# Weight conversion behind the first maxima, MLP's Relu and squares half a step later, and head 6's sums ahead of head 7's

## The chip, the cores and the metric

The kernel runs on one NeuronCore of a Trainium2 chip. Its engines are TensorE (PE, the matrix unit), VectorE (DVE), ScalarE (ACT), GpSimd (POOL), and SyncE (SP), which issues most of the DMAs. The metric is the device time of one launch in microseconds; below, a median of three runs.

## The reference

Eight batches of eight heads of attention with a decay, over 576 positions of 64 channels, are followed by an MLP on the 4608 tokens of 512 channels:

```python
scores = scale * np.matmul(q, k.transpose(0, 1, 3, 2))
cum = np.cumsum(np.log(np.clip(f, 0.0001, 1.0)), axis=-1)
decay = cum[:, :, :, None] - cum[:, :, None, :]
scores = np.where(causal, -1000000000.0, scores + decay)
scores = scores - np.max(scores, axis=-1, keepdims=True)
attn = np.exp(scores)
attn = attn / (np.sum(attn, axis=-1, keepdims=True) + 1e-09)
x = np.matmul(attn, v)                    # then heads beside each other: 4608 x 512
h = np.maximum(x @ w_in, 0.0)             # 512 x 2048, weights given in float64
out = h * h @ w_out                       # 2048 x 512
```

## The kernel before, in words

The work of the 64 heads is cut into units, six a head (`NU`): each is one block of scores against up to 448 queries, its exponential, and, two units later (`LAG`), its product with the values. Unit `n` is the step of one long traced loop, from `-12` to the end; what a unit issues on PE, ACT, DVE and POOL stays in exactly the order in which the loop wrote it (`in_order`, L18). So an instruction that waits holds up everything behind it on its engine. SP's DMAs are placed by the scheduler.

A softmax row's maximum is computed one head ahead, by six pieces of scores (`max_units`, L363) that DVE reduces (L380). A piece's PSUM bank is free for another product when L380 is done. For the first ten heads the maxima are then turned on PE (`turn_maxima`, L403) and copied by ACT (L407) into a row of the operand of the scores, which run in full float32 there (L419); from head 10 on the scores are made of two rounded products (L421, L424), and from head 16 on the probabilities are split too: ACT casts (L451), DVE subtracts (L452), and PE makes three products (L462 to L464) into one accumulator bank that ACT empties (L497, L498). POOL masks those probabilities (L438).

The sums of a pair of heads are inverted and spread through DMAs (`finish`, L500), and POOL multiplies (L519). Only for heads 6 and 7, the last of the first batch, is this done on PE and DVE at once (`finish_here`, L523): one-column matmuls (L533) turn the sums into columns, DVE inverts, and matmuls against an identity (L548) spread them.

The 32 weight tiles are given in float64. Each is loaded by SP (L195), made a float32 by ACT (magnitude, L206) and DVE (L229, L234, L237, L240), and split into a high part (ACT, L211) and a low part (DVE, L217). `weight_ops` (L187) is a generator whose yields are steps, four to a weight; `RATES` (L654) says how many steps each unit takes: first number for units -12 to -7, second for -3 to -1, third to the unit at which the first batch is ready (53), fourth from there until all are done.

The MLP runs in half steps that `fill` (L690) spreads over the units by a goal that depends on the unit's number alone. An even half (`mlp1`, L576) makes one 128 x 256 block of `x @ w_in` from twelve matmuls (L582) into the single bank 4, then Relu on ACT (L590), the square twice, on DVE (L591) and rounded on ACT (L592), and their difference on DVE (L593). An odd half (`mlp2`, L596) makes the second product of the step before by six matmuls (L605). Twelve matmuls on constants before the first score (`spin`, L751) and 36 at the very start keep PE's clock up.

While the first two chunks of the MLP share the weights that are ready, scores and maxima have two PSUM banks; from the third chunk on they have four.

Of the kernel before, what the change touches and what calls it, by code (L numbers as in the profile page):

```python
# [9 lines left out]
F32 = mybir.dt.float32  # L10
# [24 lines left out]
def decay_attention_relu2_kernel(  # L35
# [18 lines left out]
    nc = tc.nc  # L54

    NH, D, _, S = qk.shape
    P = 2 * D
# [26 lines left out]
    def bank(use):  # L84

        turn = banks[use] or banks["s"]
        b = turn.pop(0)
        turn.append(b)
        return psum.tile([P, 512], F32, name=f"bank{b}")
# [97 lines left out]
    def weight_ops():  # L187

        staged, done = {}, {}

        def stage():
            i = len(staged)
            if i < NW:
                raw = staged[i] = wk.tile([P, 2 * DM], I32, name=f"w{i}", bufs=1)
                nc.sync.dma_start(out=raw, in_=(w_in, w_out)[i % 2][i // 2].bitcast(I32))  # L195

        def words(i):
            w = staged[i].rearrange("p (n t) -> p n t", t=2)
            return w[:, :, 0], w[:, :, 1]

        mags = {}

        def magnitude(i):
            if i < NW:
                mags[i] = wk.tile([P, DM], F32, name="wmag", bufs=1)
                nc.scalar.activation(out=mags[i], in_=words(i)[1].bitcast(F32), func=AF.Abs)  # L206

        def high_part(i):
            if i >= 0:
                hl = wk.tile([P, 2, DM], F32R, name=f"w{i}", bufs=1)  # L210
                nc.scalar.copy(out=hl[:, 0], in_=done[i])  # L211
                done[i] = done[i], hl

        def low_part(i):
            if i >= 0:
                w, hl = done.pop(i)
                nc.vector.tensor_tensor(out=hl[:, 1], in0=w, in1=hl[:, 0].bitcast(F32), op=ALU.subtract)  # L217
                split_w.append(hl)

        stage()  # L220
        yield
        magnitude(0)
        stage()
        yield
        for i in range(NW):
            low, high = words(i)
            mag = mags.pop(i)

            nc.vector.tensor_scalar(mag, mag, MAG_LOW, MAG_HIGH, ALU.max, ALU.min)  # L229
            yield  # L230
            w = done[i] = wk.tile([P, DM], F32, name="osb")
            wi = w.bitcast(I32)

            nc.vector.tensor_scalar(wi, mag.bitcast(I32), 3, 0x3FFFFFFF, ALU.logical_shift_left, ALU.bitwise_and)  # L234
            high_part(i - 1)
            yield
            nc.vector.scalar_tensor_tensor(wi, high, -0x40000000, wi, ALU.bitwise_and, ALU.bitwise_or)  # L237
            magnitude(i + 1)
            yield
            nc.vector.scalar_tensor_tensor(wi, low, 29, wi, ALU.logical_shift_right, ALU.bitwise_or)  # L240
            low_part(i - 1)
            while len(staged) < min(i + 1 + DEPTH, NW):
                stage()
            yield
        high_part(NW - 1)
        yield
        low_part(NW - 1)
        yield
# [271 lines left out]
            del state[h], state[h - 1]  # L520


    def finish_here(h, part):  # L523

        st = state[h]
        cuts = [min(j * P, S - P) for j in range(NJ)]
        if part == 0:
            one = vhs[0][:, 0, D:D + 1].bitcast(F32)
            c = st["cmp"] = wk.tile([P, 2 * NJ], F32, name="cmp")
            for i in range(2):  # L530
                ps = bank("m")
                for j, q0 in enumerate(cuts):
                    nc.tensor.matmul(  # L533
                        ps[:, j:j + 1], st["den"][i * D:i * D + 1, q0:q0 + P],
                        one[i * D:i * D + 1], start=True, stop=True,
                    )
                nc.vector.tensor_scalar_add(c[:, i * NJ:(i + 1) * NJ], ps[:, :NJ], EPS)
            nc.vector.reciprocal(out=c, in_=c)
        if part == 1:
            c = st["cmp"]  # L540
            x = xts[h // H][:, (h % H) // 2, :]
            for a, b in ((0, 512), (512, S)):
                ps = bank("m")
                for j, q0 in enumerate(cuts):
                    if a <= j * P < b:
                        m = min(S - j * P, P)
                        for i in range(2):
                            nc.tensor.matmul(  # L548
                                ps[i * D:(i + 1) * D, j * P - a:j * P - a + m],
                                c[:, i * NJ + j:i * NJ + j + 1].broadcast_to([P, D]),  # L550
                                eye_r[:, P - m:].bitcast(F32), start=True, stop=True,
                            )
                nc.vector.tensor_tensor(out=x[:, a:b], in0=x[:, a:b], in1=ps[:, :b - a], op=ALU.mult)
            del state[h], state[h - 1]
# [3 lines left out]
    def split_x(c, finished):  # L558
# [14 lines left out]
            t0 = t1  # L573
        mst["x", c] = (xh, xl), t0

    def mlp1(c, fc):  # L576
        xh, xl = mst["x", c][0]
        ph = bank("h")
        w = split_w[2 * fc].rearrange("p s (c f) -> p s c f", f=P)
        for k, (s, x) in enumerate(((1, xh), (0, xh), (0, xl))):  # L580
            for cc in range(NCC):
                nc.tensor.matmul(  # L582
                    ph[:, :T], w[:, s, cc], x[:, cc, :],
                    start=(cc == 0 and k == 0), stop=(cc == NCC - 1 and k == 2),
                )
        r = wk.tile([P, T], F32, name="r", bufs=1)
        g = wk.tile([P, T], F32, name="g", bufs=1)
        gh = wk.tile([P, T], F32R, name="gh")
        gl = wk.tile([P, T], F32R, name="gl")
        nc.scalar.activation(out=r, in_=ph[:, :T], func=AF.Relu)  # L590
        nc.vector.tensor_tensor(out=g, in0=r, in1=r, op=ALU.mult)  # L591
        nc.scalar.activation(out=gh, in_=r, func=AF.Square)  # L592
        nc.vector.tensor_tensor(out=gl, in0=g, in1=gh.bitcast(F32), op=ALU.subtract)  # L593
        mst["g", c, fc] = (gh, gl)
# [30 lines left out]
                return None  # L625

    def mlp_half(finished):
        if halves[0] % 2:
            if len(steps) > 1:
                mlp2(*steps[-2])  # L630
# [20 lines left out]

    RATES = (1, 1.6, 0.8, 1.8)  # L654
    LAG = 2
    NA = H * NU

# [21 lines left out]
    fins = {}  # L679
    for h in range(1, NH, 2):  # L680
        if h == H - 1:
            for part in range(2):
                fins.setdefault((h + 1) * NU + 2 + part, []).append((finish_here, h, part))
            continue
        for part in range(4):
            fins.setdefault(fin(h, part), []).append((finish, h, part))
# [75 lines left out]
    load_cum(0, rounded[0].k)  # L762
    load_cum(0, whole[0].k, D + 1)
    store_cum()
    load_rounded(1, False)
    load_whole(1)
    load_cum(1, rounded[1].k)
# [26 lines left out]
    convert(1 << 20)  # L794
    while halves[0] < 2 * NCHUNK * NF:
        mlp_half(B)
    mlp2(*steps[-1])
    in_order(tc, [getattr(mybir.EngineType, e) for e in ("PE", "Activation", "DVE", "Pool")], start)

# [38 lines left out]
```

## Time and profile before

| | us |
|---|---|
| median of three runs (1216.88 to 1219.87) | 1217.59 |
| profiled execution, its own time | 1216.4 |
| its span, first to last instruction | 1214.7 |
| PE busy | 1182.6 (97%) |
| DVE busy | 784.1 (65%) |
| ACT busy | 696.0 (57%) |
| POOL busy | 304.6 (25%) |
| granted PE clock, mean | 0.99 |

Busy time of PE is modelled, since matmuls overlap; what a matmul really takes of PE is read from the distance of starts. A row of the timeline gives start and duration in us, the engine (PEld is PE's weight load, SPq an issue of a DMA), the line, the operation, output and inputs by the program's names, and in brackets the idle time of the engine before it and what ended it. Line numbers in rows of the profile before are those of the kernel before.

### The profile page before, as it was taken

To read this page: it belongs to the slowest core of one execution; us is meant where nothing else is said; L and a number is where in the kernel's file an instruction comes from. 1 tells how busy PE (TensorE), PEld (TensorE's weight loads), DVE (VectorE), ACT (ScalarE), POOL (GpSimd) and SP (SyncE) were. 2 spreads that over 40 slices of the span, in tenths; PEclk is the share of its full clock that TensorE was granted. 3 is DMA by queue.
4 is the path that set the end of the run, shared out by engine and by line. 5 is a ranking of instruction groups with operands and counts; after the bars stand their busy time and mean duration, and the time that the engine had idled before them with its cause. 6 is when DMAs were issued, how large, how long until landed. Compare 5 with 4: busy or idle time off the path is not lost. (4 is left out here: it accounts for less than half of the span.)

```text
span 1214.7 us, 23295 instructions
## 1 busy us (share of the span) xinstructions
PE 1182.6 (97%) x7786; PEld 1043.8 (86%) x7786; DVE 784.1 (65%) x2095; ACT 696.0 (57%) x1716; POOL 304.6 (25%) x511
## 2 busy tenths in 40 slices
PE   6999999989999999999999999999999999999998
PEld 3668777779998899999999989998899899999997
DVE  5878888666666767665655766667666667533332
ACT  2875555546665666656556566666666666533232
POOL 2110000113334333322322333333333333200000
PEclk8998999989999999999999999999999999999999
DMA  7785522221212111121120211212121212000000
GB/s 214 201 229 173 137 52 55 69 53 42 59 42 54 41 50 42 42 54 24 42 59 16 54 34 48 51 42 60 36 55 32 54 42 59 11 28 10 9 19 18
DMA packets 109799, 73.33 MB, mean 60 GB/s; under 512 B 90720, under 2 KB 90720, under 8 KB 109680
## 3 DMA queue, kind: packets, MB, share of 16 engines
q1 hardware_dynamic: 108880, 68.90, 22.1%
q0 software_dynamic: 800, 2.95, 1.0%
q8 instruction: 62, 1.02, 0.3%
q14 instruction: 57, 0.47, 0.1%
HBM read 58.71 MB, written 9.87 MB: 56 GB/s over the span
## 5 line engine op out<-in xcount | busy, mean ns | idle before, releaser
L605 PE MATMUL bank<-w,gh 128*128 128x512 f32 x1152 | 414.0, 400 | 0.0
L582 PE MATMUL bank<-xh,w 128*128 128x256 f32 x2304 | 329.9, 286 | 1.6 <-ACT w L211 1.6
L582 PEld LDWEIGHTS bank<-xh,w 128*128 128x128 f32 x2304 | 301.6, 190 | 9.8 <-ACT w L211 2.2
L452 DVE TENSOR_TENSOR pl<-p,ph 128x320 fp32r<-128x320 f32 (+4 forms) x288 | 175.6, 610 | 193.4 <-ACT ph L451 188.2
L605 PEld LDWEIGHTS bank<-w,gh 128*128 128x128 f32 x1152 | 217.5, 189 | 38.4
L590 ACT ACTIVATE r<-bank 128x256 f32<-128x256 f32 x288 | 110.4, 383 | 221.5 <-PE bank L582 183.3
L605 PE MATMUL bank<-w,gl 128*128 128x512 f32 x576 | 227.0, 394 | 0.2 <-DVE gl L593 0.2
L591 DVE TENSOR_TENSOR g<-r 128x256 f32<-128x256 f32 x288 | 123.9, 430 | 134.2 <-ACT r L590 133.3
L451 ACT CAST ph<-p 128x320 fp32r<-128x320 f32 (+4 forms) x288 | 119.4, 415 | 145.2 <-POOL p L438 103.3
L582 PE MATMUL bank<-xl,w 128*128 128x256 f32 x1152 | 184.4, 282 | 0.0
L438 POOL TENSOR_SCALAR_AFFINE_SELECT p<-p 128x128 f32<-128x128 f32 (+1 forms) x240 | 77.3, 322 | 423.2 <-ACT p L436 328.9
L582 PEld LDWEIGHTS bank<-xl,w 128*128 128x128 f32 x1152 | 158.2, 191 | 0.0
L593 DVE TENSOR_TENSOR gl<-g,gh 128x256 fp32r<-128x256 f32 x288 | 126.8, 440 | 35.0 <-PE bank L605 0.5
L436 ACT ACTIVATE p<-bank 128x320 f32<-128x320 f32 (+4 forms) x288 | 111.4, 387 | 64.6 <-PE bank L424 52.8
L380 DVE CUSTOM_DVE_ANT_0 bank<-bank,mz 128x256 f32<-128x256 f32 (+4 forms) x320 | 133.3, 432 | 18.6 <-PE bank L372 17.1
L372 PE MATMUL bank<-rk 66*128 66x320 f32 (+4 forms) x384 | 110.7, 317 | 22.6 <-DVE tcol L380 16.3
L592 ACT ACTIVATE gh<-r 128x256 fp32r<-128x256 f32 x288 | 120.5, 418 | 9.2
L605 PEld LDWEIGHTS bank<-w,gl 128*128 128x128 f32 x576 | 109.2, 190 | 14.4 <-DVE gl L593 0.9
L372 PEld LDWEIGHTS bank<-rk 66*128 66x128 f32 (+1 forms) x384 | 67.3, 181 | 40.5 <-DVE tcol L380 21.2
L424 PE MATMUL bank<-rl 128*128 128x320 f32 x324 | 95.2, 294 | 0.0
L462 PE MATMUL bank<-pl,vh 128*65 128x320 f32 (+4 forms) x336 | 93.1, 277 | 1.9 <-ACT den L498 1.9
L421 PE MATMUL bank<-rk 67*128 67x320 f32 x324 | 93.4, 288 | 0.1
(97 smaller groups left out, 1483.8 us busy)
## 6 DMA issues: line engine op xcount, KB each, us to landing
qkraw<-in_qk SPq DMA_DIRECT2D x54, 288.0 KB
v<-in_v SPq DMA_DIRECT2D x64, 160.0 KB
out<-osb SPq DMA_DIRECT2D x36, 256.0 KB
den<-rdr SPq DMA_DIRECT2D x62, 144.0 KB
w<-in_w_in SPq DMA_DIRECT2D x16, 512.0 KB
w<-in_w_out SPq DMA_DIRECT2D x16, 512.0 KB
rk<-tcol SPq DMA_DIRECT2D x216, 0.5 KB
rl<-in_qk SPq DMA_DIRECT2D x10, 288.0 KB
```

The source lines that it names most:

```text
L372: nc.tensor.matmul(ps[:m, :n], st["r2"][:D + 2, q0:q0 + m], st["kl0"][:D + 2, k0:k0 + n], start=True, stop=True,)
L380: nc.vector.tensor_tensor_reduce(out=ps[:m, :n], in0=ps[:m, :n], in1=mz[:m, mo:mo + n], op0=ALU.add, op1=ALU.min, scale=-1.0, scalar=init, ...
L424: nc.tensor.matmul(ps[:kn, :n], st["l2"][:, k0:k0 + kn], st["r1"][:, q0:q1], start=False, stop=not added,)
L436: nc.scalar.activation(out=p[:kn, :n], in_=ps[:kn, :n], func=AF.Exp, scale=SCALE)
L451: nc.scalar.copy(out=ph[:kn, :n], in_=p[:kn, :n])
L452: nc.vector.tensor_tensor(out=pl[:kn, :n], in0=p[:kn, :n], in1=ph[:kn, :n].bitcast(F32), op=ALU.subtract,)
L582: nc.tensor.matmul(ph[:, :T], w[:, s, cc], x[:, cc, :], start=(cc == 0 and k == 0), stop=(cc == NCC - 1 and k == 2),)
L590: nc.scalar.activation(out=r, in_=ph[:, :T], func=AF.Relu)
L591: nc.vector.tensor_tensor(out=g, in0=r, in1=r, op=ALU.mult)
L592: nc.scalar.activation(out=gh, in_=r, func=AF.Square)
L593: nc.vector.tensor_tensor(out=gl, in0=g, in1=gh.bitcast(F32), op=ALU.subtract)
L605: nc.tensor.matmul(po, g[:, ts], w[:, s], start=(fc == 0 and k == 0), stop=(fc == NF - 1 and k == 2),)
```

## The change

Four edits. The second weight is staged a step earlier, ahead of the loads of head 1, by one call more of `convert`; its magnitude is taken a step later, after the first weight's last bit operation (L240, now L242); and the rates are changed, so that the steps ahead of the first score become 4 instead of 10.8 and those between it and unit 53 more. `mlp1` only issues its matmuls; Relu, squares and difference are moved into `bend`, which the next half step calls first. In `finish_here` each head's sums are now a part of their own: head 6's at unit 46, head 7's at unit 50, the spreading at unit 51 as before.

```diff
@@ weight_ops
         stage()
         yield
+        stage()
+        yield
         magnitude(0)
-        stage()
         yield
@@ in its loop over the weights
-            magnitude(i + 1)
+            if i:
+                magnitude(i + 1)
             yield
             nc.vector.scalar_tensor_tensor(wi, low, 29, wi, ALU.logical_shift_right, ALU.bitwise_or)
             low_part(i - 1)
+            if i == 0:
+                magnitude(1)
@@ finish_here
-        if part == 0:
+        if part < 2:
             one = vhs[0][:, 0, D:D + 1].bitcast(F32)
-            c = st["cmp"] = wk.tile([P, 2 * NJ], F32, name="cmp")
-            for i in range(2):
-                ps = bank("m")
-                for j, q0 in enumerate(cuts):
-                    nc.tensor.matmul(
-                        ps[:, j:j + 1], st["den"][i * D:i * D + 1, q0:q0 + P],
-                        one[i * D:i * D + 1], start=True, stop=True,
-                    )
-                nc.vector.tensor_scalar_add(c[:, i * NJ:(i + 1) * NJ], ps[:, :NJ], EPS)
+            if part == 0:
+                inv.append(wk.tile([P, 2 * NJ], F32, name="cmp"))
+            c = inv[0][:, part * NJ:(part + 1) * NJ]
+            ps = bank("m")
+            o = part * D
+            for j, q0 in enumerate(cuts):
+                nc.tensor.matmul(
+                    ps[:, j:j + 1], st["den"][o:o + 1, q0:q0 + P], one[o:o + 1], start=True, stop=True,
+                )
+            nc.vector.tensor_scalar_add(c, ps[:, :NJ], EPS)
             nc.vector.reciprocal(out=c, in_=c)
-        if part == 1:
+        if part == 2:
@@ mlp1, after its matmuls: what follows is bend's now
+        bent.append((c, fc, ph))
+
+    def bend():
+
+        if not bent:
+            return
+        c, fc, ph = bent.pop()
         r = wk.tile([P, T], F32, name="r", bufs=1)
...
     def mlp_half(finished):
+        bend()
         if halves[0] % 2:
...
-    RATES = (1, 1.6, 0.8, 1.8)
+    RATES = (0.67, 0, 0.93, 1.8)
...
-            for part in range(2):
-                fins.setdefault((h + 1) * NU + 2 + part, []).append((finish_here, h, part))
+            for part, n in enumerate((h * NU + 4, (h + 1) * NU + 2, (h + 1) * NU + 3)):
+                fins.setdefault(n, []).append((finish_here, h - (part == 0), part))
...
     store_cum()
+    convert(1)
     load_rounded(1, False)
```

How it moves instructions is seen at three places. The first is DVE ahead of the first maximum (L380 before, L384 now; `wmag` is the magnitude, `osb` the float32 being made, `tcol` the maximum). Before:

```order
L229 TENSOR_SCALAR wmag<-wmag 128x512
L234 TENSOR_SCALAR osb<-wmag 128x512
L237 SCALAR_TENSOR_TENSOR osb<-w_143,osb 128x512
L240 SCALAR_TENSOR_TENSOR osb<-w_143,osb 128x512
L229 TENSOR_SCALAR wmag<-wmag 128x512
L380 ISA bank_187,tcol<-bank_187,mz 128x256
L380 ISA tcol 128x1
```

Now:

```order
L230 TENSOR_SCALAR wmag<-wmag 128x512
L235 TENSOR_SCALAR osb<-wmag 128x512
L238 SCALAR_TENSOR_TENSOR osb<-w_143,osb 128x512
L384 ISA bank_177,tcol<-bank_177,mz 128x256
L384 ISA tcol 128x1
L384 ISA bank_181,p<-bank_181,mz,tcol 128x320
```

L240 of the first weight and L229 of the second no longer stand ahead of head 0's maxima; they come after the first pieces of head 1's.

The second is DVE at head 12's first maximum, while weights are converted (`g` and `gl` are the square and the difference of the MLP; L325 is a part of the operands' preparation, L329 now). Before:

```order
L318 CAST rk_79<-qkraw 64x576
L229 TENSOR_SCALAR wmag<-wmag 128x512
L234 TENSOR_SCALAR osb<-wmag 128x512
L591 TENSOR_TENSOR g<-r 128x256
L593 TENSOR_TENSOR gl<-g,gh 128x256
L325 TENSOR_TENSOR rl<-qkraw,rk_79 64x576
L380 ISA bank_1672,tcol<-bank_1672,mz 128x256
L380 ISA tcol 128x1
L237 SCALAR_TENSOR_TENSOR osb<-w_1369,osb 128x512
```

Now:

```order
L322 CAST rk_79<-qkraw 64x576
L230 TENSOR_SCALAR wmag<-wmag 128x512
L607 TENSOR_TENSOR g<-r 128x256
L609 TENSOR_TENSOR gl<-g,gh 128x256
L235 TENSOR_SCALAR osb<-wmag 128x512
L329 TENSOR_TENSOR rl<-qkraw,rk_79 64x576
L384 ISA bank_1665,tcol<-bank_1665,mz 128x256
L384 ISA tcol 128x1
L238 SCALAR_TENSOR_TENSOR osb<-w_1349,osb 128x512
```

The pair `g`, `gl` ahead of the maximum belongs to the product that left PE just before, in the first listing, and to the one before that, in the second, where L235 (L234 before) has come behind it.

The third is ACT in head 20, from its fourth unit's exponential (66 x 64) to its sixth's (128 x 256); `r` and `gh` are the MLP's Relu and rounded square. Before:

```order
L436 ACTIVATE p<-bank_3812 66x64
L451 CAST ph<-p 66x64
L590 ACTIVATE r<-bank_3838 128x256
L592 ACTIVATE gh<-r 128x256
L436 ACTIVATE p<-bank_3859 128x448
L451 CAST ph<-p 128x448
L436 ACTIVATE p<-bank_3887 128x256
L451 CAST ph<-p 128x256
```

Now:

```order
L440 ACTIVATE p<-bank_3813 66x64
L455 CAST ph<-p 66x64
L440 ACTIVATE p<-bank_3852 128x448
L455 CAST ph<-p 128x448
L606 ACTIVATE r<-bank_3839 128x256
L608 ACTIVATE gh<-r 128x256
L440 ACTIVATE p<-bank_3888 128x256
L455 CAST ph<-p 128x256
```

Relu and rounded square went behind the exponential and the cast of the 448-wide unit. On PE nothing else changes its place but the one-column matmuls of `finish_here`; on POOL nothing does. On SP the second weight's load moves ahead of head 1's.

More of the change, by code (lines that the diff above doesn't have):

```diff
@@ L520, in finish @@
             del state[h], state[h - 1]
+    inv = []
     def finish_here(h, part):
@@ L526, in finish_here @@
         cuts = [min(j * P, S - P) for j in range(NJ)]
-        if part == 0:
+        if part < 2:
             one = vhs[0][:, 0, D:D + 1].bitcast(F32)
-            c = st["cmp"] = wk.tile([P, 2 * NJ], F32, name="cmp")
-            for i in range(2):
-                ps = bank("m")
-                for j, q0 in enumerate(cuts):
-                    nc.tensor.matmul(
-                        ps[:, j:j + 1], st["den"][i * D:i * D + 1, q0:q0 + P],
-                        one[i * D:i * D + 1], start=True, stop=True,
-                    )
-                nc.vector.tensor_scalar_add(c[:, i * NJ:(i + 1) * NJ], ps[:, :NJ], EPS)
+            if part == 0:
[8 more added lines that the diff above has]
+            nc.vector.tensor_scalar_add(c, ps[:, :NJ], EPS)
             nc.vector.reciprocal(out=c, in_=c)
-        if part == 1:
-            c = st["cmp"]
+        if part == 2:
+            c = inv[0]
             x = xts[h // H][:, (h % H) // 2, :]
@@ L574, in split_x @@
         mst["x", c] = (xh, xl), t0
+    bent = []
     def mlp1(c, fc):
@@ L796, in decay_attention_relu2_kernel @@
         mlp_half(B)
+    bend()
     mlp2(*steps[-1])
```

## The prediction

> **What bounds the kernel now.** I read the busy times by stage first, then who waits for whom on TensorE (PE), then the timeline at each place so found. A row of the first view gives a stretch in us, its length, busy us and instructions of PE, of PE's weight loads, of DVE, ACT and POOL, the granted PE clock and the DMA share. The last row is from the chain of waits.
>
> ```profile
> 12.38:15.79 3.41, 0.75 (x4) 0.28 (x3) 0.00 (x0) 0.00 (x0) 0.00 (x0) 1.00 0.64 156
> 15.79:26.03 10.24, 5.64 (x20) 3.33 (x20) 5.66 (x18) 2.54 (x5) 0.69 (x2) 0.50 0.89 299
> 25.35:86.49 61.14, 59.69 (x346) 41.13 (x345) 50.24 (x158) 47.06 (x117) 9.35 (x18) 0.99 0.82 210
> 90.88:97.71 6.83, 6.83 (x39) 5.17 (x35) 4.79 (x8) 1.96 (x5) 0.20 (x2) 0.50 0.41 161
> 244.48:247.89 3.41, 1.80 (x10) 1.24 (x9) 3.08 (x6) 1.10 (x4) 0.43 (x3) 1.00 0.00 0
> 263.27:1058.00 794.73, 790.82 (x5386) 721.05 (x5385) 530.61 (x1432) 502.25 (x1250) 271.49 (x430) 1.00 0.19 44
> 1206.63 1.43 PE bank L582 x12
> ```
>
> From 263 us on PE is busy for 790.8 of 794.7 us, and the chain shows twelve 256-column matmuls passing in 1.43 us, 0.119 each. That part is bound by PE's own work, which the change leaves alone. What can be won lies ahead of 263 us, where the waits of PE stand (us in total, times, longest); the second row is the first one confined to 90 to 270 us.
>
> ```profile
> PE bank L372 <- DVE tcol L380: 16.3, 7, 7.1
> PE bank L372 <- DVE tcol L380: 9.2, 6, 1.8
> PE bank L582 <- ACT w L211: 1.6, 1, 1.6
> PE bank L372 <- DVE rk L318: 1.6, 1, 1.6
> DVE g L591 <- ACT r L590: 133.3, 109, 2.4
> ```
>
> One wait of 7.1 us lies at the start, six make 9.2 us while weights are converted beside the first MLP chunks, and DVE itself stands 133 us behind the MLP's Relu.
>
> **The start: conversion leaves the first maxima's way.**
>
> ```profile
> 11.80 0.36 PE L372 MATMUL bank<-rk 66*128 66x256 f32 x1 [1.25 <-DMA rk<-qkraw]
> 14.78 0.36 SPq L195 DMA_DIRECT2D w<-in_w_out  x1
> 18.68 0.66 ACT L206 ACTIVATE wmag<-w 128x512 f32<-128x512 f32 x1 [10.65 <-DMA w<-in_w_out]
> 19.37 0.43 DVE L229 TENSOR_SCALAR wmag<-wmag 128x512 f32<-128x512 f32 x1 [8.52 <-ACT wmag L206]
> 19.71 0.43 DVE L380 CUSTOM_DVE_ANT_0 bank<-bank,mz 128x256 f32<-128x256 f32 x1
> 22.54 0.76 PE L403 MATMUL bank<-p 128*65 128x128 f32 x5
> 23.11 2.45 PE L751 MATMUL bank<-mz 128*128 128x448 bf16 x6
> 23.33 0.68 ACT L407 COPY rl<-bank 1x512 f32<-1x512 f32 x2 [3.99 <-PE bank L403]
> 25.35 1.04 PE L419 MATMUL bank<-rl 67*128 67x320 f32 x2
> ```
>
> Head 0's first maximum could run at 11.80 + 0.36 = 12.16, but on DVE it stands behind L229 of weight 1, which waits for ACT's magnitude, which waits for a weight that SP issued at 14.78 only. In the new order that L229 follows two heads' maxima. From the first L380 to the turning matmuls L403 took 22.54 - 19.71 = 2.83 us, from there to the end of the copies L407 24.01 - 22.54 = 1.47, and the score L419 then waited out six warming matmuls, 2.45 us at half clock. At full clock these take 1.2: 12.16 + 2.83 = 14.99 for L403, 16.5 for the copies, 15.6 + 1.2 = 16.8 for the warming matmuls, so the score starts near 16.8 instead of 25.35. I take 8.3 us. Moved on SP: the second weight's load goes ahead of head 1's keys, queries, sums and head 0's values. It took at most 18.68 - 14.78 = 3.9 us, and this is the most that head 1's rows or the values can come later than they would; they are wanted within two units of the first score (the fifty units from 25.35 to 86.49 take 1.2 us each). So the term lies between 8.5 - 3.9 = 4.6 and 8.5.
>
> The half clock follows the idle time: PE was busy 0.75 of 3.41 us before 15.79, and the clock was 0.50 for the next 10.24 us. With maxima and warming matmuls running through 12 to 17 us I expect it to stay at 1.00.
>
> **The debt: 0.93 conversion steps per unit instead of 0.8.** Fifty-three units make 6.9 more steps; five DVE instructions share four steps, the dearest and the cheapest of them being
>
> ```profile
> L217 DVE TENSOR_TENSOR w<-osb,w 128x512 fp32r<-128x512 f32 x32 | 23.1, 721 | 0.6 <-ACT w L211 0.5
> L229 DVE TENSOR_SCALAR wmag<-wmag 128x512 f32<-128x512 f32 x32 | 14.6, 456 | 8.5 <-ACT wmag L206 8.5
> ```
>
> so a step is 0.57 to 0.90 us, 0.75 in the middle, and 6.9 of them 5.2 us. DVE was busy 50.24 of 61.14 us between 25.35 and 86.49; it goes from 82% to about 90% there. Its cover is 10.9 us of idle time and the three PSUM banks that the maxima rotate through. PE's loss lies between 0 and 5.2; I take 1.5, nearer to nothing because PE was busy 59.69 of 61.14 with 82%. At the unit where the MLP starts both orders have done nearly the same steps (54.2 of 132, 55.3 of 133), so nothing is owed later.
>
> **Head 6's sums earlier.**
>
> ```profile
> 87.51 1.97 PE L533 MATMUL bank<-vh,den 1*128 1x1 f32 x20
> 90.47 1.83 PE L548 MATMUL bank<-p,cmp 128*64 128x128 f32 x20
> 92.19 0.82 DVE L553 TENSOR_TENSOR xt<-xt,bank 128x512 f32<-128x512 f32 x2 [1.48 <-PE bank L548]
> 94.25 1.23 DVE L570 TENSOR_TENSOR xl<-xt,xh 128x1024 fp32r<-128x1024 f32 x1
> 96.43 1.77 PE L582 MATMUL bank<-xh,w 128*128 128x256 f32 x8
> ```
>
> The twenty one-column matmuls (1.97 us) are not removed, only halved in two places; one more reciprocal costs 0.2 us of DVE, which 10.9 us of idle time hide. But these 2 us in which the array streams almost nothing precede 90.88, where the clock falls to 0.50 for 6.83 us. Work that fills such a stretch loses half, 3.4 us. Split four units apart, neither half holds PE for more than 1 us. Late next is the first MLP input: from 92.19 DVE owes L553, a conversion, the cast and L570 (0.82 + 0.69 + 0.69 + 1.23), while PE's 4.1 us from L548's end (92.30) to L582 shrink to 2.1; the cast is about even, L570 shows some 0.5. I take 2.9, between 0 and 3.4.
>
> **Relu and squares a half step later, while weights are converted.** One of the six stalls, on DVE unless marked:
>
> ```profile
> 136.70 0.38 ACT L590 ACTIVATE r<-bank 128x256 f32<-128x256 f32 x1 [0.22 <-PE bank L582]
> 137.29 0.41 DVE L591 TENSOR_TENSOR g<-r 128x256 f32<-128x256 f32 x1
> 137.83 0.42 DVE L593 TENSOR_TENSOR gl<-g,gh 128x256 fp32r<-128x256 f32 x1
> 138.84 0.42 DVE L380 CUSTOM_DVE_ANT_0 bank<-bank,mz 128x256 f32<-128x256 f32 x1
> 139.37 0.41 PE L372 MATMUL bank<-rk 66*128 66x320 f32 x1 [1.83 <-DVE tcol L380]
> ```
>
> The maximum stood behind the square and difference of a product that had just left PE: 0.83 us of work plus the wait for Relu, up to 1 us. In the new order the pair before it is the previous product's, long ready. Four of the six stalls have this form, 0.9 to 1.9 us each, some 5.2 in sum; but the displaced pair now stands before a later maximum of the same head, with DVE nearly full, and gives 1.2 of it back. I take 4, between 1 and 6. The other two follow a DVE run that waits for the division of head 15 (L318's 1.6 us, the row of 244.48 with PE at 1.80 of 3.41), and keep their order: 0, with the 3.4 us of a half-clock stretch as the upper bound. The last weight (1.6 us on L582) is converted one pair and one Relu wait earlier: 1.5, between 0 and 1.6.
>
> **The same half step in the bound stage.** The gain and the price in one head of 16 and later:
>
> ```profile
> 300.06 0.36 ACT L498 COPY den<-bank 1x256 f32<-1x256 f32 x1
> 300.26 0.28 PE L424 MATMUL bank<-rl 128*128 128x192 f32 x1
> 300.47 0.36 PE L462 MATMUL bank<-pl,vh 128*65 128x320 f32 x1
> 306.55 0.36 PE L424 MATMUL bank<-rl 128*128 128x448 f32 x1
> 307.33 0.53 ACT L436 ACTIVATE p<-bank 128x448 f32<-128x448 f32 x1
> 308.31 0.57 ACT L451 CAST ph<-p 128x448 fp32r<-128x448 f32 x1 [0.45 <-POOL p L438]
> 308.91 1.19 PE L582 MATMUL bank<-xh,w 128*128 128x256 f32 x8
> ```
>
> L424's 192 columns pass in 0.09, yet L462 starts 0.21 after it: it waits 0.12 for the one bank that the copy L498 frees 0.05 earlier. Without Relu and square ahead, that copy ends 0.7 us sooner; 48 heads make 5.8 us. Against it: the product's bank is also single, so the next L582 waits for Relu, and at 306 us Relu now stands behind the exponential and cast of the 448-wide unit. Exponential from 306.9 to 307.5, mask and its wait 0.45, cast 0.57, Relu 0.38 (all by rows of the old order), release 0.05: 308.95, while L582 would be ready at 308.91 - 0.12 = 308.79. That is 0.16 late, 7.7 us over 48 heads. I take a loss of 1, between a loss of 8 and a gain of 5.8. What waits behind the Relu on ACT (square, next exponential) has 1 us of slack before the second product.
>
> Sum against the profiled execution's 1216.4 (span 1214.7 and 1.7 around it): 8.3 - 1.5 + 2.9 + 4 + 1.5 - 1 = 14.2, so 1202.2. The runs' median of 1217.59 is 1.2 above that execution, so I forecast 1203.
>
> **The rivals.**
> *The bank is free in time (1195).* If mask and cast follow the earlier exponential without the 0.45 us, the 7.7 us are never paid, and +5.8 stand instead of -1; 1203 - 7 = 1196, and 1195 with a little of the half-clock stretch at 247.9. For it: the mask alone takes 0.3. Against: POOL was the releaser of that cast even with Relu ahead.
> *The half-clock stretch at 91 is not the change's to win (1206).* The low windows sit on a grid of 3.41 us (15.79, 90.88 and 247.89 are whole steps apart). 2 us of idle PE trip it only if they fall into one window; where they don't, before has no such loss, and 2.9 us are missing. The Trainium skill (TensorE: Matmul & The Clock Gate, Part 1) says so: the window of 3413 ns is free-running and doesn't start with the kernel; the grid here agrees with the length, and one execution can't show whether it moves.
> *DVE's debt and the queue eat half the start (1209).* At 90% DVE costs PE 5 instead of 1.5, and head 1's rows or the values come 2 to 3 us late behind the weight: 1203 + 3.5 + 2.5. For it: DMA at 0.82 already; against: beyond the first rows, no DMA stands among PE's waits now.
> *The single bank of the MLP's first product becomes the bound (1231, slower).* Place: L582 after Relu, at two places in each of 48 heads. At 0.4 us each it is 38 us instead of the 9 or so in which I have counted it, +28. It decides from 0.25 us at each place, 24 us, on. Against: at the other place (300 us) only a cast stands between the copy L498, which ends 0.7 us sooner, and the Relu.
> *The stalls only move (1213 to 1217).* Every DVE wait that is removed returns at the next maximum, and the start's gain is lost to a later load. Against: PE is the bound behind it, and what comes sooner to it stays sooner.
>
> **How the numbers follow.** Forecast 0.50, free bank 0.17, clock stretch 0.13, debt and queue 0.12, single bank 0.05, only moved 0.03. The forecast's own range is 1198 to 1207; 1193 to 1212 takes in free bank, clock and debt. A measurement here tells a change from none at about 0.3%, 3.7 us: below 1213.9 is faster. The cases below that have 0.92 to 0.93, the last rival is split between no change and faster, the single bank is slower from 0.25 us at a place: 0.92, 0.04, 0.04.
>
> **What would show it.** Right: the first L419 near 17 us and no 7 us wait of L372; clock 1.00 at 12 to 26 and 88 to 98 us; four of the six waits for L380 under 1 us; L582 waiting for ACT r in most heads, 0.1 to 0.2 us each. Wrong: the first score after 20 us, a wait for a DMA before 30 us, DVE idle behind Relu as before, or a bound stage more than 8 us longer than 794.7.

## The result, and the profile after

The changed kernel takes 1208.98 us (median of 4 runs, 1208.21 to 1210.55) against 1217.49 (1216.88 to 1219.87) in the same comparison: a ratio of 0.9929, 95% interval 0.9905 to 0.9953. It is faster, by 8.5 us where 14.2 were forecast. The profiled execution took 1208.21 us, with a span of 1206.5 against 1214.7 before. One run of a later experiment (values loaded earlier; 1223.11 us at clock 0.985) counts as slow and is left out of its ratio.

New lines sit a little lower in the file: the maxima's matmul L372 is now L376 and its reduction L384, the scores' first matmul is L423 (whole heads), L425 and L428 (split heads), values L487 and L466 to L468, the MLP's products L591 and L621, Relu L606, squares L607 and L608, values' load L306, sums' rows L286, sums' copies for the division L512.

Who waited for whom in the profile after (engine, line, what it waited for; us in total, times, longest):

```profile
PE bank L376 <- DVE tcol L384: 8.4, 8, 1.7
PE bank L591 <- ACT r L606: 5.1, 8, 0.8
PE bank L376 <- DMA rk<-cum_dr: 2.6, 1, 2.6
PE bank L487 <- DMA v<-in_v: 2.0, 1, 2.0
PE bank L487 <- ACT w L211: 1.2, 1, 1.2
DVE g L607 <- ACT r L606: 101.7, 62, 3.6
```

The 7.1 us at the start are gone, and DVE stands 102 us behind Relu instead of 133. Three kinds of wait are new: PE for a row of sums, PE for values (the 1.2 us at L487 are put down to ACT's copy of a weight, which is no operand of that matmul; an execution further down names the values there), and the MLP's first product for Relu.

Stretches of the profile after (us; length, then busy us of PE, PE's weight loads, DVE, ACT, POOL, granted clock, DMA share, GB/s):

```profile
17.88:21.29 3.41, 1.56 (x9) 1.32 (x10) 0.99 (x5) 0.42 (x2) 0.00 (x0) 1.00 1.07 350
21.29:24.70 3.41, 3.41 (x13) 2.22 (x12) 3.30 (x14) 1.61 (x5) 0.91 (x2) 0.50 0.69 217
16.44:85.84 69.40, 62.71 (x356) 42.91 (x355) 53.41 (x163) 48.91 (x119) 9.22 (x18) 0.98 0.81 205
88.00:98.00 10.00, 10.00 (x79) 7.63 (x79) 8.57 (x22) 5.82 (x14) 0.20 (x2) 1.00 0.46 137
239.74:243.16 3.42, 1.63 (x10) 1.26 (x11) 2.81 (x9) 0.94 (x3) 0.29 (x1) 1.00 0.40 89
243.16:246.57 3.41, 3.41 (x16) 3.17 (x15) 1.49 (x6) 0.80 (x2) 0.00 (x0) 0.50 0.02 0
```

The half clock is down to two stretches of 3.41 us, where before had 10.24, 6.83 and 6.83. But the fifty units from the first score on take 69.40 us; before they took 61.14, with PE busy 59.69 of them.

The start of the same unit in both profiles (its score's first matmul on PE) shows where time came and went:

| stage (units) | won, us | forecast |
|---|---|---|
| to the first score, 25.35 before, 16.44 after | +8.9 | +8.3 |
| unit 0 to 50 | -8.3 | -1.5 |
| 50 to 54, the sums of heads 6 and 7 | +3.5 | +2.9 |
| 54 to 96, MLP while weights are converted | +0.8 | +4 |
| 96 to 98, the last weight | +1.9 | +1.5 |
| 98 to 110, the two kept stalls | +0.4 | 0 |
| 110 to the end | +1.0 | -1 |
| sum | +8.2 | +14.2 |

The start came as forecast and was then paid back within fifty units. In these rows of PE and SP one sees by what:

```profile
14.57 0.23 SPq L286 DMA_DIRECT2D rk<-cum_dr  x1
16.44 0.70 PE L423 MATMUL bank<-rl 67*128 67x320 f32 x2
19.73 0.50 PE L376 MATMUL bank<-rk 66*128 66x256 f32 x2 [2.59 <-DMA rk<-cum_dr]
34.84 3.73 SPq L512 DMA_DIRECT2D cmp<-den  x2
38.62 0.58 SPq L195 DMA_DIRECT2D w<-in_w_out  x1
39.30 0.58 SPq L306 DMA_DIRECT2D v<-in_v  x1
60.55 1.11 SPq L520 DMA_DIRECT2D den<-rdr  x2
62.84 0.59 SPq L306 DMA_DIRECT2D v<-in_v  x1
70.50 0.72 PE L487 MATMUL bank<-ph,v 128*65 128x320 f32 x2 [2.01 <-DMA v<-in_v]
```

The row of sums for head 1 was issued at 14.57 and used at 19.73. The values used from unit 20 on were issued at 39.30, behind two copies of sums that held SP's queue for 3.73 us. Before, the same values were issued ahead of the second of these copies, at 36.59, although unit 18 came 5 us later (46.46 instead of 41.12). Those of head 6, used from unit 38 on, were issued at 62.84, behind the reading back of sums (60.55), 2.0 us ahead of the start of unit 36; before, they were issued at 56.52, 11.3 us ahead of it:

```profile
35.50 0.52 SPq L508 DMA_DIRECT2D cmp<-den  x1
36.12 0.38 SPq L282 DMA_DIRECT2D rk<-cum_dr  x1
36.59 0.57 SPq L302 DMA_DIRECT2D v<-in_v  x1
56.52 0.57 SPq L302 DMA_DIRECT2D v<-in_v  x1
```

By the distances of unit starts, the 8.3 us are 2.5 for head 1's row (units 0 to 2), 1.6 in the stretch at half clock (2 to 6), 1.35 and 2.05 at the two waits for values (18 to 24, 36 to 42), and 1.35 for head 6's sums, whose one-column matmuls now stand in unit 46 (2.76 us, before 1.41). All other units together won 0.6, DVE's debt included. So 1.35 us of this row belong to the sums, whose row of the table shows only what they win.

### The profile page after: what moved, and what is told of

The parts are those of the page before. It is cut to its first block, busy times and chain, and to the rows that moved or that the text cites. A ratio compares the mean times of both kernels' runs of the same rounds, so it can differ in the third digit from the quotient of the medians.

```text
span 1206.5 us, 23195 instructions
## 1 busy us (share of the span) xinstructions
PE 1178.1 (98%) x7786; PEld 1040.9 (86%) x7786; DVE 784.9 (65%) x2096; ACT 684.6 (57%) x1716; POOL 316.9 (26%) x511
## 5 line engine op out<-in xcount | busy, mean ns | idle before, releaser
L621 PE MATMUL bank<-w,gh 128*128 128x512 f32 x1152 | 413.5, 399 | 0.0
L591 PE MATMUL bank<-xh,w 128*128 128x256 f32 x2304 | 331.6, 286 | 5.3 <-ACT r L606 5.1
L591 PEld LDWEIGHTS bank<-xh,w 128*128 128x128 f32 x2304 | 300.1, 189 | 16.8 <-ACT r L606 9.3
L621 PEld LDWEIGHTS bank<-w,gh 128*128 128x128 f32 x1152 | 217.5, 189 | 37.9
L621 PE MATMUL bank<-w,gl 128*128 128x512 f32 x576 | 227.1, 394 | 0.2 <-DVE gl L609 0.2
L607 DVE TENSOR_TENSOR g<-r 128x256 f32<-128x256 f32 x288 | 124.3, 432 | 102.0 <-ACT r L606 101.7
L442 POOL TENSOR_SCALAR_AFFINE_SELECT p<-p 128x128 f32<-128x128 f32 (+1 forms) x240 | 85.9, 358 | 396.1 <-ACT p L440 328.2
L606 ACT ACTIVATE r<-bank 128x256 f32<-128x256 f32 x288 | 109.7, 381 | 137.1 <-PE bank L591 124.5
L591 PE MATMUL bank<-xl,w 128*128 128x256 f32 x1152 | 184.8, 283 | 0.0
L384 DVE CUSTOM_DVE_ANT_0 bank<-bank,mz 128x256 f32<-128x256 f32 (+4 forms) x320 | 133.6, 431 | 50.6 <-PE bank L376 50.2
L609 DVE TENSOR_TENSOR gl<-g,gh 128x256 fp32r<-128x256 f32 x288 | 139.1, 483 | 34.4 <-PE bank L621 1.0
L591 PEld LDWEIGHTS bank<-xl,w 128*128 128x128 f32 x1152 | 158.5, 191 | 0.2 <-DVE xl L577 0.2
L608 ACT ACTIVATE gh<-r 128x256 fp32r<-128x256 f32 x288 | 120.4, 418 | 9.2
L376 PE MATMUL bank<-rk 66*128 66x320 f32 (+4 forms) x384 | 109.1, 314 | 13.4 <-DVE tcol L384 8.4
L621 PEld LDWEIGHTS bank<-w,gl 128*128 128x128 f32 x576 | 109.2, 190 | 15.0 <-DVE gl L609 1.7
L428 PE MATMUL bank<-rl 128*128 128x320 f32 x324 | 95.1, 294 | 0.0
L425 PE MATMUL bank<-rk 67*128 67x320 f32 x324 | 93.4, 288 | 0.0
L376 PEld LDWEIGHTS bank<-rk 66*128 66x128 f32 (+1 forms) x384 | 67.1, 181 | 30.4 <-DVE tcol L384 12.8
L466 PE MATMUL bank<-pl,vh 128*65 128x320 f32 (+4 forms) x336 | 91.3, 272 | 0.0
```

The lines of the kernel that those rows point to most:

```text
L376: nc.tensor.matmul(ps[:m, :n], st["r2"][:D + 2, q0:q0 + m], st["kl0"][:D + 2, k0:k0 + n], start=True, stop=True,)
L384: nc.vector.tensor_tensor_reduce(out=ps[:m, :n], in0=ps[:m, :n], in1=mz[:m, mo:mo + n], op0=ALU.add, op1=ALU.min, scale=-1.0, scalar=init, ...
L428: nc.tensor.matmul(ps[:kn, :n], st["l2"][:, k0:k0 + kn], st["r1"][:, q0:q1], start=False, stop=not added,)
L591: nc.tensor.matmul(ph[:, :T], w[:, s, cc], x[:, cc, :], start=(cc == 0 and k == 0), stop=(cc == NCC - 1 and k == 2),)
L621: nc.tensor.matmul(po, g[:, ts], w[:, s], start=(fc == 0 and k == 0), stop=(fc == NF - 1 and k == 2),)
```

## The experiments

Three groups of runs, each with its own runs of the kernel before beside it: 35, 21 and 17 of them, medians 1216.55, 1216.35 and 1217.69, with granted clocks between 0.981 and 0.996. Ratios are to these; the clock is the mean over a kernel's runs.

| kernel | median, us | ratio, 95% interval | clock |
|---|---|---|---|
| only the conversion's edit | 1216.43 | 1.0005 (0.9978 to 1.0031) | 0.991 |
| only Relu and squares later | 1214.42 | 0.9981 (0.9953 to 1.0009) | 0.991 |
| only head 6's sums | 1215.97 | 1.0004 (0.9978 to 1.0030) | 0.991 |
| change, values loaded earlier | 1207.70 | 0.9947 (0.9922 to 0.9972) | 0.994 |
| change, once more | 1210.32 | 0.9947 (0.9922 to 0.9973) | 0.994 |
| change + 38 matmuls on a constant | 1203.27 | 0.9892 (0.9862 to 0.9921) | 0.9995 |
| change, second weight later | 1208.04 | 0.9930 (0.9901 to 0.9959) | 0.996 |
| change, Relu ahead of the cast | 1202.79 | 0.9886 (0.9858 to 0.9914) | 0.995 |
| before + 44 matmuls on a constant | 1213.72 | 0.9973 (0.9954 to 0.9991) | 0.995 |
| change + constant + Relu ahead | 1197.87 | 0.9842 (0.9814 to 0.9870) | 0.998 |
| the same, weight later, values earlier | 1196.76 | 0.9838 (0.9808 to 0.9868) | 0.998 |

**One part at a time.** First, the conversion's edit on the kernel before: the second weight staged early, its magnitude later, the new rates.

```diff
-    RATES = (1, 1.6, 0.8, 1.8)
+    RATES = (0.67, 0, 0.93, 1.8)
...
     store_cum()
+    convert(1)
     load_rounded(1, False)
```

> Only the conversion's part of the change (second weight staged ahead of head 1's loads, magnitude of it later, rates 0.67, 0, 0.93); Relu and squares and the sums of heads 6 and 7 as before. My theory: the first score comes at 16.4 us as in the changed kernel, but values and head 1's rows come late on SP's queue, and at unit 50 less than 1.5 us is left of it: 1216 to 1217.5. Rival, DVE's debt: the same loss, but PE waits for L380, not for a DMA. Rival, the loss needs the other parts: 1209 to 1211, with 6 us or more left at unit 50.

Then Relu and squares alone, by `bent` and `bend()`:

> Only Relu, squares and difference a half step later. My theory: it is worth what the changed kernel gained after unit 54, about 4 us: 1212.5 to 1214.5, with about 1 us of it behind unit 110. Rival, single bank of the first product: nothing or a loss, 1217 to 1220, with over 6 us of waits of the first product for Relu. Rival, the gain after unit 54 came from another state of the conversion: 1216 to 1218.

Then the sums alone, by the three-part `finish_here`:

> Only head 6's sums turned and inverted four units ahead of head 7's. My theory: the half clock at 91 us goes, 3 to 3.5 us: 1213.5 to 1215. Rival, the windows of the clock move from run to run and before pays for them only at times: a profile without a half clock at 91 in either kernel and medians within 1.5 us, 1216 to 1218.

No part by itself can be told from the kernel before. The medians win 0.1, 2.1 and 0.6 us, each uncertain by some 3, and 2.8 in sum, where all three together win 6.0 in the runs below; what each is worth within the change stays open. The conversion's trace has the first score at 16.58, unit 50 still 6.1 us early, unit 96 only 0.6 early. So its expected time came in another way than expected: less than 1.5 us was to be left at unit 50, and the loss lies behind it, 2.2 us in units 50 to 54 and 3.2 in 54 to 96. The stretches of that trace:

```profile
79.99:83.41 3.42, 2.98 (x26) 2.22 (x23) 2.71 (x10) 2.23 (x6) 0.00 (x0) 1.00 1.06 263
83.41:93.65 10.24, 10.24 (x52) 7.59 (x52) 6.17 (x16) 2.49 (x6) 0.20 (x2) 0.50 0.50 137
158.50:161.91 3.41, 1.68 (x10) 0.99 (x9) 3.05 (x11) 1.70 (x5) 0.00 (x0) 1.00 0.28 87
161.91:165.33 3.42, 3.42 (x15) 3.14 (x14) 0.67 (x1) 0.67 (x1) 1.52 (x1) 0.50 0.41 87
```

The start's half clock is gone, in which PE had been idle for 4.6 of 10.24 us, and there is as much of it in places where PE has work: 10.24 us at the sums (with sixteen of the sums' one-column matmuls in the stretch ahead), 3.41 more than before, and a new one at 162. By half of what they last, these two explain some 1.7 us each of the two losses; the rest, 0.5 and 1.5, stays open. With Relu alone the trace shows neither the stretch at 91 nor that at 248, although nothing was changed at the sums. So where the half clock falls in one execution is no property of the kernel; comparing two profiles credits or charges a change with it.

**The change once more, unaltered**, to see how its time depends on the clock.

> The change once more, unaltered, beside many runs of the kernel before. Two readings of its gain. Clock: the granted clock falls to a half for whole stretches of 3.41 us after a stretch in which PE waited a lot, and how many such stretches an execution has decides its time; then the mean clock of these runs lies above that of the kernel before (0.9896 over 35 runs), at 0.994 to 0.997, time falls with it by 0.4 to 0.5 us for each us at half clock in either kernel, and the median is 1208 to 1210. Work: the gain is in waits that are gone, whatever the clock; then runs of equal clock differ by 7 to 8 us.

Its 12 runs reach from 1203.44 us at clock 0.998 to 1216.57 at 0.990; those of before beside it from 1211.33 at 0.995 to 1228.69 at 0.981. A straight line through either set gives 0.55 and 0.43 us of time for each us at half clock (twice the missing clock times the span). Both readings are borne out in part. The clock sets the spread within a kernel. At equal mean clock, 0.992 to 0.995, the change's runs (1208 to 1213) lie 2 to 4 us below those of before (1211 to 1217), and before has 10 us of its half clock at the start, where PE is idle for 4.6 of them. If these cost nothing, which no run shows by itself, before would have 10 us less than the change of those that cost 0.43, and the distance would be 6 to 8 us. Two stretches of its profile at half clock, each behind the one that tripped it, stand where the first profile of the same kernel had full clock:

```profile
41.43:44.84 3.41, 1.57 (x13) 1.11 (x12) 2.11 (x9) 1.56 (x5) 0.00 (x0) 1.00 1.08 197
44.84:48.25 3.41, 3.41 (x11) 1.78 (x11) 2.89 (x9) 1.44 (x3) 0.51 (x1) 0.50 0.76 238
218.92:222.33 3.41, 1.66 (x13) 1.34 (x12) 2.77 (x9) 1.01 (x4) 0.43 (x1) 1.00 0.01 1
222.33:225.74 3.41, 3.41 (x12) 2.92 (x12) 2.45 (x9) 1.38 (x3) 0.00 (x0) 0.50 0.02 0
```

It also names the wait at unit 20 for what it is: for values, 1.8 us.

**The change, with PE kept busy where it waits longest.** The constant goes into the bank that the next real matmul overwrites.

```diff
+    WARM = {76: 4, 80: 4, 92: 6, 98: 7, 104: 7}
+
     def score(h, u):
...
         ps = bank("s")
+        for _ in range(WARM.get(h * NU + u, 0)):
+            nc.tensor.matmul(ps[:, :MW], mz[:, :P], mz, start=True, stop=True)
@@ max_units, ahead of the matmul of head 1's first piece
+            for _ in range(10 if h == 1 and q0 + m == S and k0 == 0 else 0):
+                nc.tensor.matmul(ps[:, :MW], mz[:, :P], mz, start=True, stop=True)
```

> The change, and where PE waits longest it multiplies a constant into the bank that it writes next: 10 such matmuls ahead of head 1's first maximum, 4 to 7 ahead of a score in five of the stalls while weights are converted (38 in all, 0.19 us each at full clock, 7 us). Nothing useful is added. Clock theory: the half-clock stretches at 21.29 and 243.16 us go, the mean clock rises to 0.997 or more, the median falls 3 us under the change's own, and the spread narrows. Work theory: the waits remain as long, the matmuls fill them or lengthen them, so 0 to 3 us slower than the change.

Seven us less than the change beside it, where 3 were expected, from work that computes nothing. All six runs lie between 1202.09 and 1204.73, at clock 0.999 or 1.000. Its trace at the places in question:

```profile
16.64:25.00 8.36, 8.36 (x49) 5.52 (x48) 5.37 (x18) 4.13 (x10) 0.62 (x2) 1.00 1.05 318
16.64:81.79 65.15, 62.80 (x367) 43.01 (x365) 52.45 (x162) 48.58 (x119) 8.69 (x18) 1.00 0.87 216
240.00:243.20 3.20, 3.20 (x21) 2.62 (x21) 2.00 (x7) 2.34 (x6) 0.24 (x1) 1.00 0.17 45
```

By the clock, 15.2 us at half clock (0.0063 x 2 x 1209) become 1.2, and 14 us at half clock are 7 us of work: the clock accounts for the whole difference. The two traces agree: the change's has three stretches of 3.41 us at half clock ahead of its end, this one none, and its span is 5.0 us shorter. So some 7 us of the change's median in this group are the clock's.

**The same on the kernel before**: 4 matmuls on the constant ahead of each half of the sums, `WARM = {68: 6, 76: 6, 92: 6, 98: 4, 104: 7}`, 7 ahead of head 18's first piece.

> The kernel before the change, with 44 matmuls on a constant that add nothing to the result: 4 ahead of each half of head 6's and 7's sums at 87 us, 4 to 7 ahead of five scores and of one maximum at which PE waits, between 136 and 250 us. The start is left alone: its 10.24 us at half clock pass while PE waits anyway. Clock theory: the stretches at 90.88 and 247.89 us go, mean clock 0.995 (the start's stretch alone), median 1210 to 1211 and a spread of some 4 us; so 5 to 6 us of the old kernel's time were the clock's, and what is left to the change at equal clock is the distance to the other kernel with such matmuls (1203.3), some 7 us. Work theory: 0 to 5 us slower than before.

```profile
14.78:25.02 10.24, 4.77 (x17) 2.71 (x18) 5.11 (x17) 2.48 (x5) 0.69 (x2) 0.50 0.80 278
25.11:262.00 236.89, 229.67 (x1440) 180.52 (x1440) 189.04 (x521) 141.91 (x345) 23.91 (x51) 1.00 0.49 129
```

The two later stretches are gone, as expected, and the start's is kept. The median came out 3 us above the 1210 to 1211 expected: units 50 to 52 take 7.2 us, and 5.1 at full clock without the 8 matmuls (the trace with Relu alone), so 2.1 us are the price of these, and three of the twelve runs had more at half clock (0.991 to 0.994). With both kernels at full clock beyond the first score, the change is worth 1213.72 - 1203.27 = 10.4 us, less 2.1 for those matmuls, less a little for the three runs and less up to 1.3 because the two groups differ by that in the kernel before: some 7 to 8, across two groups of runs.

**The queue.** The second weight loaded behind head 0's values:

```diff
-        stage()
-        yield
+        hooks.append(stage)
         stage()
         yield
...
+    at(-3, 0, lambda: hooks[0]())
...
     store_cum()
-    convert(1)
```

> The change, but the second weight is loaded behind head 0's values, not ahead of head 1's rows. Queue theory: PE's wait of 2.6 us for head 1's sums row at 17 to 20 us shrinks below 1, unit 6 starts 2 us sooner than 26.79, and some 2 us arrive at the end: 1206 to 1207. Rival, the debt decides: the second weight's conversion then waits for its load on DVE, in front of the maxima, and unit 50 starts no sooner than 85.8: no change, 1209.

And values earlier: in the change, heads 1 to 9 load theirs four units sooner.

```diff
-        at((h - 1) * NU + VLOAD, 1, load_v, h)
+        at((h - 1) * NU + (VLOAD if split else VLOAD - 4), 1, load_v, h)
```

> The changed kernel with the loads of the values of heads 1 to 9 traced four units earlier. My theory, late values: the waits of L487 at units 20 and 38 (1.3 and 2.2 us) go, 1205 to 1206.5. Rival, the DMA engines are full and the time only moves to the key loads behind: 1208 to 1210. Rival, DVE's debt: no change, 1209, since L487 is not what is late.

Waits of PE between 16 and 90 us, first with the values earlier, then in the unaltered change of the other group, then with the weight later:

```profile
PE bank L376 <- DMA rk<-cum_dr: 1.5, 1, 1.5
PE bank L376 <- DVE p L384: 1.0, 2, 0.8
```

```profile
PE bank L487 <- DMA v<-in_v: 2.4, 2, 1.8
PE bank L376 <- DMA rk<-cum_dr: 1.4, 1, 1.4
```

```profile
PE bank L487 <- DMA v<-in_v: 2.4, 4, 1.0
```

Either edit removes its own wait: values earlier leaves none for values; with the weight later none for the row of sums is left, and unit 2 starts at 18.02 instead of 19.98. Neither median can be told from the change's, whose interval holds both. In the trace with the weight later unit 50 starts 1.2 us ahead of the change's in the same group, where the wait for the row was 1.4 (2.6 in the first profile); waits of 1.0 us or less, mostly for values, stand at seven places. In the trace with values earlier unit 50 starts at 87.55, later than in either trace of the change (85.84 and 83.30): it has 13.65 us at half clock from 19.25 on. So the queue theory is right on the cause of the two waits; what removing them is worth, some 2 us by these medians, is not settled.

**Relu ahead of the cast.** In each half step `bend()` is called before the last exponential is split:

```diff
         while halves[0] < min(goal, limit):
+            bend()
             split_last()
             if not mlp_half(b):
```

> The change, but in each half step Relu and square are issued ahead of the cast of the exponentials, not behind it. Single-bank theory: the waits of L591 for ACT r (5.1 us, 8 of them, and 5.5 us in the bound stage) go, 2 to 5 us won: 1204 to 1207. Rival, the cast is what the second product needs next: pl and the products wait as long behind Relu instead, 0 to 3 us slower than the change.

1202.79 against 1210.32 in the same group, 7.5 us less and better than the range expected. Waits of PE from 262 to 1060 us, before, in the change, and here:

```profile
PE bank L462 <- ACT den L498: 1.9, 6, 0.4
PE bank L372 <- DVE rk L340: 1.8, 3, 1.3
```

```profile
PE bank L591 <- ACT r L606: 3.9, 6, 0.8
PE bank L376 <- DVE rk L344: 1.3, 3, 0.7
```

```profile
PE bank L376 <- DVE rk L344: 2.3, 3, 1.1
PE bank L621 <- DVE gl L609: 0.2, 1, 0.2
```

Waits below some 0.2 us are not in these rows, but the mean unit lengths of heads 20 to 62 hold them (us):

| | third unit of a head | sixth unit | whole head |
|---|---|---|---|
| before | 3.99 | 3.30 | 17.40 |
| change | 3.87 | 3.42 | 17.37 |
| Relu ahead of the cast | 3.82 | 3.30 | 17.25 |

The change takes 0.12 from the third unit, where the second product waited for the bank of the sums' copy, and adds 0.12 to the sixth, where the next product waits for Relu behind a 448-wide cast. Both are mean values over 43 heads, and they come with the edit: the other three traces without it (conversion, sums, before with the constant) have 3.98 to 4.00 and 3.30, the five others with it and with the cast first 3.87 to 3.88 and 3.43. With Relu ahead, the gain stays and the price is gone. From unit 110 to the end the three profiles take 946.9, 945.9 and 940.7 us; the change's second one takes 946.8, so 6.1 of the 7.5 us are won there.

**Both.** The constant's 38 matmuls and Relu ahead, in one kernel; then with the second weight later and values earlier as well.

> The change, with Relu and square ahead of the cast, and with the 38 matmuls on a constant. If the two gains are of different places (the bound stage from 262 us on, and the clock ahead of it): 1196 to 1198, clock 0.999. If they overlap: 1201.

> As the one with Relu ahead and the constant's matmuls, and the second weight loaded behind head 0's values, heads 1 to 9 having their values loaded four units earlier. Queue theory: the waits for values and for head 1's row are gone, unit 50 starts near 80 instead of 81.8 us, and 1 to 3 us arrive at the end: 1194 to 1196. Debt theory: DVE's conversions set unit 50's start anyway: no change against the one without.

1197.87 and 1196.76: of the 7.0 and 7.5 us that the two edits won singly, 12.4 arrive together. The first kernel's five runs lie 8 us apart, at clocks from 0.995 to 1.000, and its profile has 10.24 us at half clock between 68 and 90 us: with Relu ahead the 38 matmuls did not hold the clock in every execution. Either kernel beats the kernel before by 20 us and the change by 11 or more. The two can't be told apart; unit 50 stands at 82.41 us in the second's trace, not at 80, with new waits, for keys (1.8 us) and by ACT's copy of a weight (1.0):

```profile
PE bank L378 <- DVE tcol L386: 2.6, 7, 0.7
PE bank L429 <- DMA rl<-in_qk: 1.8, 2, 1.4
PE bank L597 <- ACT r L612: 1.3, 3, 0.6
PE bank L429 <- ACT w L212: 1.0, 1, 1.0
```

That trace has no half clock ahead of its end, and a span of 1192.3 us.

## Why the prediction was right, and where it was not

The direction and the wide range (1193 to 1212) held; the likeliest case was 6 us too good, and its own range, 1198 to 1207, was missed by 2. One of the signs that were to show it wrong came, a wait for a DMA before 30 us. The time is that of the third rival (1209, a chance of 0.12), and of its mechanism one half, the queue. Two terms came too good, the start with its debt (6.8 forecast, 2.0 measured) and Relu later (4 and 0.8); that the bound stage came 2 us better than forecast hid a part of it, which was luck.

*The start, 8.3.* Right to the first score (8.9), wrong as a term of the sum. The step that failed is the bound for what was moved on SP: "this is the most that head 1's rows or the values can come later", from the 3.9 us of one weight. It priced the one load that the edit moves, and held the rest of the queue to its old times. What counts is not how much later a load comes, but whether it comes as much sooner as the units that need it. Head 1's row did not, and neither did the values, which SP issued in a new order, those of head 3 behind copies that wait for ACT: 2.5 + 3.4 us. With 1.6 us at half clock after the first of these waits the net at unit 50 is 0.65, or 2.0 without the sums' share, below the lower bound of 4.6 - 1.5. In three other traces of the change's order (once more, constant, Relu ahead) unit 50 stands 3.2, 4.7 and 1.7 us ahead of before, 4.5, 6.1 and 3.0 without the sums' share, and with the conversion's edit alone 6.1; so the first profile was a poor draw, and 8.3 too much in any. Over all traces, the fifty units take 60.9 to 63.4 us with the old start (four traces) and 63.8 to 71.7 with the new one (nine).

*The debt, -1.5.* Nothing of it is seen: the units without a wait for a DMA, half clock or the sums won 0.6 in all, and DVE was busy 53.41 of 69.40 us, 77% and not 90%. The third rival had it at 5; its other half, the queue, was twice the 2.5 it named.

*The half clock after idle time.* "I expect it to stay at 1.00" held to 21.29 us and then failed: PE was busy 1.56 of 3.41 us while it waited for head 1's row.

*Head 6's sums, 2.9.* 3.5 in units 50 to 54, no half clock at 88 to 98 us, but 1.35 paid in unit 46, so 2.2 in this pair. And the kernel with Relu alone has no half clock there either and wins 2.9 us in these units with the sums untouched. So at full clock the halved sums win 0.6 in unit 50 and lose 1.35 in unit 46; what they can win is half clock that an execution may or may not have. Where one step of 3.41 us holds sixteen to twenty of the one-column matmuls, the clock fell behind it in two of three traces; in the nine traces with the sums apart it fell behind one of nineteen steps that hold some. The term was read from a stretch that isn't in every execution, as the second rival said. The Trainium skill's page "TensorE: Matmul & The Clock Gate" (Part 1) has a window of 3413 ns that runs free of the kernel. The traces agree on the length (all stretches but the one that the kernel's end cuts off are of 3.41 us or whole multiples to 0.02 us), and two profiles of the changed kernel now show that it moves: their first stretches, at 21.29 and 44.84 us, are 6.9 steps apart.

*Relu later while weights are converted, 4.* Wrong in size: 0.8, and 1.0 between the two kernels kept at full clock. The step that failed is "some 5.2 in sum", less 1.2 given back. The four stalls of this form (units 68, 76, 87 and 92) went from 1.83, 1.74, 1.23 and 1.78 us to none, 0.97, 0.68 and 1.41: 3.5 won, not 5.2, since the earlier pair still stands ahead of the maximum. The displaced pair gave back 1.7 (1.05 and 0.65 at units 80 and 88, which had no stall), and the MLP's first product waits 0.7 for Relu at unit 59.

*The last weight, 1.5, and the kept stalls, 0.* 1.9 and 0.4. The first stall shrank from 1.61 to 0.49, the one at unit 98 grew from 0.99 to 1.75; the second stayed (1.59, now 1.62), and the stretch behind it fell to half clock again, for 3.41 us instead of 6.83.

*The bound stage, -1.* Right in each part: 0.12 x 48 = 5.8 was forecast for the freed bank, and the third unit won 0.117; the price was put at 0.16 a head and is 0.122. The first rival, in which the price isn't paid, describes the kernel with Relu ahead: 1202.79 in place of the change's 1210.32. The bank of the first product did not become the bound, as 0.122 us at one place in a head stays below the 0.25 at each of two that the prediction named.

What the prediction's sum left out is that both kernels' times spread by 13 to 18 us with the clock. Before spends 15 of its 25 us at half clock beyond the start, where they cost (25 by a mean clock of 0.99; 10.24 of these lie in the start of all four traces that have the old start), and the change 15 as well, in its later runs. So by this count the change won nothing of the clock there on average; the 6.0 us of that comparison (1216.35 to 1210.32) are work. In the first comparison, where its runs were at 0.996, perhaps 2 of the 8.5 are the clock's. This split is worked out from mean clocks and takes the start's 10.24 us to cost nothing; it is not shown run by run.

## What to carry to other kernels

When a start moves forward by 9 us, list every load that its first units use and ask of each whether it too moves by 9; one moved load is the smallest part of the answer. Where the clock is at half after a wait, fill the wait with idle matmuls first: 38 of them were worth 7 us here, as much as the whole change, and runs then agreed within 3 us; in another order of the same instructions they agreed within 8 only, so look at the clock again after every edit. A consumer moved later on an in-order engine frees one bank and holds another; look for the place in the order that serves both, here ahead of the cast and not behind it.

## What the runs showed of the hardware

- How often the clock falls to a half differs from run to run of one kernel: 0.981 to 0.996 in 73 runs of the kernel before, 1211 to 1229 us. In the first comparison its four runs agreed within 3 us, so that small sample hid it.
- The clock fell behind stretches in which PE was far from idle: busy 1.56 to 1.68 of 3.41 us in the rows above, and 2.98 of 3.42 where sixteen of 26 matmuls were the one-column ones of the sums. Behind 1.99 of 3.41 us, with the longest wait for values, it stayed in the change's first profile:

```profile
69.08:72.49 3.41, 1.99 (x11) 1.32 (x12) 1.99 (x10) 1.29 (x4) 0.69 (x2) 1.00 0.94 169
```

  Cut into such steps along each trace's own grid, from 8 us on and without the kernel's end, the thirteen traces show half clock behind 15 of the 16 full-clock steps with PE busy 1.64 us or less, behind 5 of the 12 with 1.66 to 1.89, and behind three of those with more, each with ten to twenty of the sums' one-column matmuls. A stall of 1.6 to 2.0 us costs a stretch, then, if the moving grid puts enough of it into one step. That this makes the spread of the runs is likely, but was not tried by itself.
- What half clock costs that falls into a wait stays open: the kernel before spends 10.24 us at half clock at its start, with PE busy 5.64 of them, and the conversion's edit alone removes these, but its runs have as low a mean clock (0.991), so its time doesn't tell.
- A wait can be put down to a semaphore that came last without being the operand (1.2 us "for ACT w" at unit 20); the next execution named the values.
